# Half of a pair's softmax blocks stay where they are: four block transfers in place of six, a copy back on two engines, a doubled buffer, and the value product 1.9 heads later

## The chip, the cores and the metric

The kernel runs on one NeuronCore of a Trainium2 chip. The metric is the device time of one execution in microseconds (us). The core has a matmul engine (PE; its weight loads are listed apart as PEld), a vector engine (DVE), a scalar engine (ACT), a general engine (POOL) and a queue engine (SP), which issues every DMA of this kernel. Each engine takes its instructions strictly in the order in which they were written out.

## The reference

The inputs are `q`, `k`, `v` of 8 batches, 8 heads, 576 tokens and 64 channels, and `s` of 8 x 8 x 576. First a causal attention with a decay bias, then a gated feed-forward block on its output:

```python
cum  = cumsum(max(s, 0))
bias = -(cum[i] - cum[j])
scores = where(j > i, -1e9, q @ k.T / 8 + min(bias, 0))
attn = softmax(scores)
x    = (attn @ v).transpose(0, 2, 1, 3).reshape(8, 576, 512)

h = gelu_tanh(x @ w_in);  u, v = halves(h)         # 576 x 512 each
v_n  = layer_norm(v) * g_ln
gated = u * (w_sg @ v_n + b_sg)                    # w_sg is 576 x 576, over tokens
return x + gated @ w_out
```

All of it is in 32-bit floating point; products in the fast 32-bit format split each operand into a high and a low part and use three matmuls for one.

## The kernel before, in words

**Heads and pairs.** There are 64 heads, worked on in 32 pairs. For one head (`scores`, line 949) the 576 queries are cut into five tiles of 64 or 128 rows, in an order of tokens that `_tokens` (line 1221) lays out from the table `BLK` (line 38), so that the five tiles need only 64, 192, 320, 448 and 576 keys each. The matmuls of a tile go to a PSUM bank (`sc`, or `sx` for the widest). Then `softmax` (line 918) runs three steps on each tile: DVE adds the mask and takes the row extreme (`mn`), ACT takes the exponential and the row sum, and DVE transposes the tile in blocks of 32 x 32 into the SBUF buffer `ex`.

**The buffers ex and pt.** After the block transpose, the 32 queries of a block lie along the columns and 32 keys along the partitions. A quarter of the partitions (32) holds one block of queries. `ex` has two halves of 1600 columns: keys whose block of 32 is even lie in the first, odd ones in the second. The product with `v` wants 64 keys on 64 neighbouring partitions. So for each pair `shuffle` (line 973) moves all eight pieces of 32 partitions x 1600 columns from `ex` to a second buffer `pt`, in six transfers issued by SP, two of which carry 64 partitions. There is one `ex` and one `pt`: the transposes of the next pair wait until the transfers have read `ex`, and the next transfers wait until the matmuls have read `pt`.

**The product with v.** `pv` (line 991) issues one uninterrupted group of 76 matmuls for a pair (38 pieces from `pieces`, line 978, each as two instructions of 64 x 64), reading `pt` and `v`, into two PSUM banks `xx`. Then four DVE multiplications scale the result by the reciprocal row sums `rb` and write `xr`, the input of the feed-forward block. The sums take a path of their own (`scales`, line 936): ACT and DVE make the reciprocals, DVE transposes them to `rt`, a DMA writes `rd` in DRAM, and two DMAs read it back spread over the partitions as `rb`. `rb` and `v` have one buffer each.

**The feed-forward block.** For each batch `ffn` (line 1014) issues units of 12 or 14 matmuls: `v_unit` (`vm`), `u_unit` (`um`), `s_unit` (`sm`) and `o_unit` (`om`), each followed by steps on ACT, DVE and POOL. The tag `u2` with `U2` = 8 buffers holds the `u` results, two small operands `xq`, the output tiles `ot`, and at the start the weights in preparation. All PSUM work but `sx` shares six banks.

**What sets the order.** Nothing is issued as the code runs. Every step is noted with a key in units of heads: for head h the loads at h - 2, the split of its operands at h - 1, the scores at h, and for the second head of a pair the shuffle at h + 0.0 and `pv` at h + 0.2 (`POS`, line 58); the feed-forward block of batch b lies between 8b + 10 and 8b + 17.6. A planner (`plan`, line 553) with a cost for each instruction (`cost`, line 382) then writes one fixed order for each engine: of the operations that are ready first by its costs, the one with the lowest key, moved by a table `SHIFT` (line 73) that has a row for each kind of operation. The keys are priorities, not times. All instructions leave through one helper, line 532, so the profile shows that line for all of them, and the work is told apart by tile names.

**Number formats.** Heads 0 to 11 use plain 32-bit matmuls with operands straight from DRAM (`kf`); later heads load `raw` and split it on ACT and POOL into `k` and `low`.

Of the kernel before, what the change touches and what calls it, by code (L numbers as in the profile page):

```python
# [18 lines left out]
BH = B * H  # L19
# [18 lines left out]
BLK = ((0, 1, 4, 5, 8), (-1, 2, 3, 6, 7))  # L38
# [12 lines left out]
U2 = 8  # L51
# [6 lines left out]
POS = dict(load=-2.0, split=-1.0, sc=(0, 0, 0, 0), sh=0.0, pv=0.2, wv=(0.1, 7.5),  # L58
# [8 lines left out]
LATENCY = [[54, 38, 39, 80, 60], [54, 35, 33, 77, 60], [54, 34, 35, 90, 60], [55, 34, 35, 80, 60], [1060] * 5]  # L67
# [3 lines left out]
ISSUE = {"pt": 645.0, "rb": 660.0, "rd": 620.0, "xq": 690.0, "kf": 580.0, "vnr": 590.0, "low": 320.0}  # L71
PHASE = (4.0, 9.0, 13.5, 61.5)
SHIFT = {
# [4 lines left out]
    "act activation sum 128x10 sum": (-10.5, 10.85, -13.42, -6.92, -0.94),  # L78
# [4 lines left out]
    "act activation vnr 64x512 vm": (-0.36, 10.23, 2.64, 2.87, -17.42),  # L83
# [4 lines left out]
    "act activation wbits 128x256 wraw": (6.84, 39.64, 82.81, 1.09, 0.4),  # L88
    "act copy cc 64x576 cf": (-0.29, 1.38, -0.29, -0.29, 0),
    "act copy cf 64x512 cps": (-4.37, -9.03, -1.53, -0.95, 0),  # L90
    "act copy cf 64x64 cps": (7.84, 7.54, 7.6, 7.91, 5.93),
    "act copy gt 128x288 u": (9.81, 3.71, 1.85, -0.84, 0),
    "act copy k 128x576 raw": (0, 0, 77.83, 273.57, 108.47),
    "act copy k 64x576 raw": (3.7, -1.3, 3.65, 9.4, 3.91),
    "act copy low 64x576 raw": (0, 0, 0.07, 0.07, -0.05),
    "act copy vt 64x512 vm": (-16.19, -21, -55.46, -44.19, -10.31),
    "act copy wi 128x256 wbits": (23, 16.76, 25.17, 25.17, 9.38),
    "act copy wo 128x256 wbits": (4.72, 6.23, 184.14, 7.43, 5.62),
    "act copy wr 128x576 wst": (-1.42, 0.68, 0.68, -2, 1.47),
    "act copy wr 1x576 wst": (0, 0.15, 0, 0.07, 0.57),  # L100
    "act copy ws 128x576 wst": (-30.29, -30.57, -26.17, -23.47, -24.47),
# [6 lines left out]
    "dve memset low 2x1152 -": (-3.2, -1.71, -1.4, 0.26, 0),  # L108
    "dve memset maska 128x64 -": (-7.53, 8.57, -3.85, 6.42, 9.89),
    "dve memset maskb 128x448 -": (0, 0, 1.51, -0.11, -0.11),  # L110
    "dve memset maskc 128x576 -": (0.13, 1.82, -3.47, -5.95, -11.1),
    "dve memset sum 128x1 -": (-0.23, -0.23, -0.23, 0.3, 0.3),
    "dve memset sum 128x52 -": (4.68, -7.24, -2.73, 9.64, 9.97),
    "dve memset vnr 33x512 -": (-0.01, 1.25, 8.26, 8.26, 4.22),
# [3 lines left out]
    "dve reciprocal sum 128x10 sum": (-0.44, 3.06, 0.25, -0.33, -3.42),  # L118
# [8 lines left out]
    "dve scalar_tensor_tensor wbits 128x256 wraw": (0, -9.07, 330.04, 137.29, 35.9),  # L127
    "dve scalar_tensor_tensor wm 128x256 wraw": (134.99, 306.62, 40.25, 11.65, 28.53),
# [3 lines left out]
    "dve tensor_scalar wbits 128x256 wbits": (-3.2, -1.01, 18.81, -10.4, 1.45),  # L132
    "dve tensor_scalar wm 128x256 wbits": (66.01, 167.25, -0.39, -4.28, -4.47),
    "dve tensor_tensor cf 64x512 cps": (2.84, 0.59, 1.89, 7.81, 0),
    "dve tensor_tensor cf 64x64 cps": (1.88, 1.2, -7.04, -10.79, -0.86),
# [3 lines left out]
    "dve tensor_tensor vnr 64x512 vm": (13.68, 14.78, 14.83, 9.99, -2.48),  # L139
# [12 lines left out]
    "dve transpose rt 128x32 sum": (-14.48, 10.59, 55.5, -72.28, -2.17),  # L152
# [198 lines left out]
class Program:  # L351
# [30 lines left out]
    def cost(self, op):  # L382
# [5 lines left out]
        d, load, port, gap = 50.0, 0.0, 0.0, 0.0  # L388
        if e == PE:
            if name == "group":  # L390
                d, load = 3000.0, 54.0
            else:
                w, m = ins
                load, n = 0.84 * w.columns(), m.columns()
# [884 lines left out]
```

## Time and profile before

| what | value |
|---|---|
| median of 3 runs | 859.82 us (856.74 to 873.91) |
| profiled execution | 855.12 us, span from the first to the last instruction 853.4 us |
| mean granted clock of PE | 0.926 of 2.4 GHz |
| DMA traffic | 123.74 MB, mean 145 GB/s |
| chain that ended last | PE 41%, DMA 27%, DVE 15%, SP's queue 6%, ACT 4% |

The chain is the work followed back from the last instruction, at each step to what released it. A busy engine is one that executes; matmuls are pipelined, so the sum of their single durations exceeds their busy time. The profiled execution took 1.7 us more than its span and is 4.7 us below the median.

### The profile page before, as it was taken

How to read it: one execution, taken by the hardware profiler on the slowest of the kernel's cores; microseconds unless marked ns; L12 is line 12 of the kernel's file. 1: busy time of each engine (PE TensorE's matmuls, PEld its weight loads, DVE VectorE, ACT ScalarE, POOL GpSimd, SP SyncE). 2: the span in 40 equal slices, each digit the busy share in tenths (PEclk: the TensorE clock that was granted, in tenths of full speed). 3: DMA queues.
4: the chain of work that ended last, by engine and by line, in shares of the span. 5: the costliest groups of instructions: out<-in, count | busy, mean ns of one | idle time of the engine just before them, and what ended most of it. 6: DMA issues, size and time to landing. Idle time of an engine off the chain costs nothing.

```text
span 853.4 us, 17656 instructions
## 1 busy us (share of the span) xinstructions
PE 720.7 (84%) x6114; PEld 643.8 (75%) x6114; DVE 576.8 (68%) x1722; ACT 496.8 (58%) x1258; POOL 442.1 (52%) x611
## 2 busy tenths in 40 slices
PE   7666684898988897888987899898986889789998
PEld 5444453888877886787876888787976889688998
DVE  6657658875678648775677667785678657683562
ACT  4443456775677556775567656784567656661440
POOL 7123368763555734556445634665445635534641
PEclk9776797899999999999999999999998999999999
DMA  7577885555555665545655456545664564544101
GB/s 182 155 194 199 224 218 147 143 148 152 157 149 150 170 165 120 144 107 159 178 157 149 122 149 175 149 114 162 171 157 106 144 171 132 138 114 94 48 29 56
DMA packets 70097, 123.74 MB, mean 145 GB/s; under 512 B 20996, under 2 KB 45700, under 8 KB 70008
## 3 DMA queue, kind: packets, MB, share of 16 engines
q1 hardware_dynamic: 70008, 122.61, 54.8%
q8 instruction: 49, 0.80, 0.4%
q14 instruction: 40, 0.33, 0.1%
HBM read 56.72 MB, written 10.26 MB: 78 GB/s over the span
## 4 chain that ended last, share of the span: by engine, by line
PE 41%; DMA 27%; DVE 15%; SPq 6%; ACT 4%; issue 3%; POOL 3%; DVEq 0%; POOLq 0%; ACTq 0%
PE om L532 9%; DMA pt<-ex 9%; PE xx L532 7%; DMA rb<-rd 7%; PE um L532 7%; SPq L532 6%; DMA rd<-rt 6%; PE vm L532 6%; PE sm L532 5%; PE sc L532 4%; DVE ex L532 3%; DVE sc L532 3%; PE sx L532 3%; DMA kf<-in_kf 2%; DVE u L532 2%
## 5 line engine op out<-in xcount | busy, mean ns | idle before, releaser
L532 ACT ACTIVATE sc<-sc,mn 128x448 f32<-128x448 f32 (+3 forms) x256 | 112.8, 440 | 112.6 <-DVE mn L532 107.3
L532 PE MATMUL xx<-pt,v 64*64 64x256 f32 (+4 forms) x2432 | 122.0, 351 | 63.8 <-DMA pt<-ex 54.9
L532 PEld LDWEIGHTS xx<-pt,v 64*64 64x64 f32 x2432 | 106.9, 160 | 81.6 <-issue 57.3
L532 DVE STREAM_TRANSPOSE ex<-sc 64x64 f32<-64x64 f32 (+3 forms) x256 | 106.5, 430 | 79.3 <-DMA pt<-ex 38.4
L532 POOL TENSOR_TENSOR k<-raw,k 64x576 fp32r<-64x576 f32 x52 | 73.6, 1416 | 134.5 <-ACT k L532 114.7
L532 PE MATMUL sm<-ws,vn 128*128 128x288 f32 x768 | 125.3, 299 | 3.6 <-ACT vn L532 3.1
L532 PE MATMUL om<-gt,wo 128*128 128x288 f32 x768 | 117.8, 301 | 6.1 <-ACT gt L532 3.1
L532 PE MATMUL um<-xs,wi 128*128 128x288 f32 x768 | 119.8, 302 | 1.5 <-DVE xr L532 1.5
L532 PE MATMUL vm<-wi,xs 128*128 128x512 f32 (+1 forms) x416 | 115.3, 409 | 2.6 <-POOL xs L532 2.4
L532 ACT CAST k<-raw 128x576 fp32r<-128x576 f32 x156 | 104.6, 670 | 22.1 <-DMA raw<-in_kq 9.0
L532 PEld LDWEIGHTS om<-gt,wo 128*128 128x128 f32 x768 | 108.7, 192 | 9.5 <-ACT gt L532 4.1
L532 PEld LDWEIGHTS sm<-ws,vn 128*128 128x128 f32 x768 | 108.7, 189 | 5.2 <-ACT vn L532 3.6
L532 PEld LDWEIGHTS um<-xs,wi 128*128 128x128 f32 x768 | 109.5, 193 | 3.4 <-PE sx L532 2.1
L532 PEld LDWEIGHTS vm<-wi,xs 128*128 128x128 f32 (+1 forms) x416 | 76.0, 190 | 18.9 <-POOL xs L532 3.4
L532 POOL TENSOR_TENSOR low<-raw,k 64x576 fp32r<-64x576 f32 x52 | 73.9, 1421 | 5.7 <-ACT k L532 2.9
L532 POOL TENSOR_TENSOR gt<-u,gt 128x288 fp32r<-128x288 f32 x64 | 50.2, 805 | 49.2 <-ACT gt L532 34.3
L532 DVE CUSTOM_DVE_ANT_0 sc<-sc,maskb 128x192 f32<-128x192 f32 (+1 forms) x128 | 62.3, 492 | 14.3 <-PE sc L532 13.9
L532 DVE SCALAR_TENSOR_TENSOR u<-u,um 128x288 f32<-128x288 f32 x128 | 55.7, 442 | 16.0 <-ACT u L532 15.0
L532 DVE SCALAR_TENSOR_TENSOR ot<-om,xr 128x288 f32<-128x288 f32 x64 | 28.7, 454 | 54.8 <-PE om L532 51.6
L532 ACT CAST low<-raw 64x576 fp32r<-64x576 f32 x52 | 34.9, 671 | 46.9 <-DMA raw<-in_kq 46.0
L532 PE MATMUL sc<-k 128*128 128x320 f32 x208 | 58.3, 286 | 4.4 <-DVE xr L532 4.3
L532 DVE TENSOR_TENSOR xr<-xx,rb 128x128 f32<-128x128 f32 (+1 forms) x128 | 31.4, 298 | 43.8 <-DMA rb<-rd 35.7
(102 smaller groups left out, 1355.8 us busy)
## 6 DMA issues: line engine op xcount, KB each, us to landing
pt<-ex SPq DMA_DIRECT2D x64, 400.0 KB
pt<-ex SPq DMA_DIRECT2D x128, 200.0 KB
v<-in_vp SPq DMA_DIRECT2D x32, 576.0 KB
raw<-in_kq SPq DMA_DIRECT2D x52, 288.0 KB
rb<-rd SPq DMA_DIRECT2D x64, 160.0 KB
out_t<-ot SPq DMA_DIRECT2D x64, 144.0 KB
wraw<-in_w_in SPq DMA_DIRECT2D x16, 256.0 KB
kf<-in_kf SPq DMA_DIRECT2D x11, 292.5 KB
```

The costliest lines, as they stand in the source:

```text
L532: real[i] = [getattr(op["eng"].real, name)(*[f(a) for a in args], **{k: f(v) for k, v in kw.items()}).ins for args, kw in calls]
```

## The change

- `ex` holds two pairs (four halves of 1600 columns), `pt` one half instead of two. The half to write is chosen by the pair's parity (`base`).
- `shuffle` moves four pieces instead of eight: two transfers from `ex` to `pt`, then two within `ex` over the pieces that were just saved, then ACT and POOL each copy one saved piece from `pt` to the place in `ex` that came free. Four pieces never move.
- `pv` reads `ex`, and its key is h + 1.9 instead of h + 0.2. The five query tiles' order of tokens (`BLK`, `_tokens`), the layout of `v` and the masks change with the new places; the pieces that had 32 columns of their own join the first wide one, so a group has 34 pieces, 68 instructions. The four DVE multiplications become two.
- The transposed reciprocals are written into a corner of `rb` instead of `rt`.
- `U2` is 5 instead of 8.
- The planner's DMA costs and the table `SHIFT` are new, so each engine's order is new as well.

```diff
-BLK = ((0, 1, 4, 5, 8), (-1, 2, 3, 6, 7))
+BLK = ((0, 1, 3, 6, 8), (-1, 2, 4, 5, 7))
-U2 = 8
+U2 = 5
-POS = dict(load=-2.0, split=-1.0, sc=(0, 0, 0, 0), sh=0.0, pv=0.2, wv=(0.1, 7.5),
+POS = dict(load=-2.0, split=-1.0, sc=(0, 0, 0, 0), sh=0.0, pv=1.9, wv=(0.1, 7.5),
...
-    xt_ = const.tile([P, 2 * RG], F32, name="ex")
-    pt_ = const.tile([P, 2 * RG], F32, name="pt")
-    nc.gpsimd.memset(xt_[64:P].pattern(0, (RG, 2), (49 * 32, 2), (1, 32)), 0.0)
+    xt_ = const.tile([P, 4 * RG], F32, name="ex")
+    pt_ = const.tile([P, RG], F32, name="pt")
+    nc.gpsimd.memset(xt_[64:P].pattern(0, (RG, 4), (49 * 32, 2), (1, 32)), 0.0)
...
-        nc.vector.transpose(out=xt_[0:r].pattern(32 * cell(h % 2, it, 0), (32, n), (RG, 2), (1, 32)), in_=o)
+        nc.vector.transpose(out=xt_[0:r].pattern(base(h) + 32 * cell(h % 2, it, 0), (32, n), (RG, 2), (1, 32)), in_=o)
+    def base(h):
+        return h // 2 % 2 * 2 * RG
...
-        rt = att.tile([P, 32], F32, name="rt", tag="rt", bufs=1)
-        nc.vector.transpose(out=rt, in_=rs)
+        rb = scale_rows[h // 2] = att.tile([P, 640], F32, name="rb", tag="rb", bufs=1)
+        nc.vector.transpose(out=rb[:, 320:352], in_=rs)
         rd = dram.tile([P, 32], F32, name="rd", tag="rd", bufs=2)
-        nc.sync.dma_start(out=rd, in_=rt)
-        rb = scale_rows[h // 2] = att.tile([P, 640], F32, name="rb", tag="rb", bufs=1)
+        nc.sync.dma_start(out=rd, in_=rb[:, 320:352])
...
     def shuffle(h):
-        for o, i, n, a, b in ((1, 0, 2, 0, 1), (1, 2, 2, 1, 1), (0, 0, 1, 0, 0), (0, 2, 1, 1, 0), (3, 1, 1, 0, 0), (3, 3, 1, 1, 0)):
-            nc.sync.dma_start(out=pt_[32 * o:32 * (o + n), RG * a:RG * a + RG],
-                              in_=xt_[32 * i:32 * (i + n), RG * b:RG * b + RG])
+        qs = [slice(32 * q, 32 * q + 32) for q in range(4)]
+        a, b = (slice(base(h) + RG * i, base(h) + RG * i + RG) for i in range(2))
+        for o, i in ((1, 0), (2, 3)):
+            nc.sync.dma_start(out=pt_[qs[o], :], in_=xt_[qs[i], a])
+        for o, i in ((0, 1), (3, 2)):
+            nc.sync.dma_start(out=xt_[qs[o], a], in_=xt_[qs[i], b])
+        nc.scalar.copy(out=xt_[qs[1], b], in_=pt_[qs[1], :])
+        nc.gpsimd.tensor_scalar(out=xt_[qs[2], b], in0=pt_[qs[2], :], scalar1=1.0, scalar2=1.0, op0=ALU.mult, op1=ALU.mult)
...
-            if m is None:
-                o, x = to.pattern(0, (1, 32)), pt_[rows].pattern(32 * cell(z, 0, 0), (1, 32))
-            else:
-                o = to.pattern(32 * m, (128, 2), (1, 32 * n))
-                x = pt_[rows].pattern(32 * cell(z, m, j), (RG, 2), (32 * (10, -12)[z], n), (1, 32))
+            o = xx[g][64 * z:64 * z + 64].pattern(32 * (m - g), (160 - 32 * g, 2), (1, 32 * n))
+            x = xt_[rows].pattern(base(h) + (1 - g) * RG + 32 * cell(z, m, j), ((-RG, RG)[g], 2), (32 * (10, -12)[z], n), (1, 32))
...
-        for g in range(2):
-            for c0, o, n in ((0, 160 * g, 160), (160, 160 * g + 352, 128)):
-                nc.vector.tensor_tensor(out=xt[:, CH * g + c0:CH * g + c0 + n], in0=xx[g][:, c0:c0 + n],
-                                        in1=rb[:, o:o + n], op=ALU.mult)
+        nc.vector.tensor_tensor(out=xt[:, 0:320], in0=xx[0][:, 0:320], in1=rb[:, 0:320], op=ALU.mult)
+        nc.vector.tensor_tensor(out=xt.pattern(320, (128, 2), (1, 128)), in0=xx[1].pattern(0, (128, 2), (1, 128)),
+                                in1=rb.pattern(352, (160, 2), (1, 128)), op=ALU.mult)
...
```

## Rows read from the trace of the kernel before

**Rows 1.** Page, part 1: busy us, share of the span, instructions.

```profile
PE 720.7 (84%) x6114; PEld 643.8 (75%) x6114; DVE 576.8 (68%) x1722; ACT 496.8 (58%) x1258; POOL 442.1 (52%) x611
```

**Rows 2.** Busy time by stage: stretch, length, engines, clock, DMA share, GB/s.

```profile
core 0: us, PE busy (x) PEld busy (x) DVE busy (x) ACT busy (x) POOL busy (x), PEclk, DMA share, GB/s
0.00:150.00 150.00, 98.55 (x628) 70.82 (x629) 100.77 (x319) 72.47 (x205) 74.04 (x104) 0.80 0.71 188
150.00:750.00 600.00, 526.42 (x4723) 482.08 (x4724) 421.82 (x1274) 390.75 (x975) 327.96 (x437) 0.95 0.57 148
750.00:853.00 103.00, 95.69 (x768) 90.91 (x766) 54.19 (x131) 33.61 (x80) 40.11 (x72) 0.98 0.24 64
```

**Rows 3.** Waits of PE, 150 to 750 us: us in total, times, longest.

```profile
PE xx L532 <- DMA pt<-ex: 46.2, 24, 11.0
PE sx L532 <- DVE ex L532: 13.0, 9, 4.2
PE xx L532 <- DVE mn L532: 4.1, 2, 2.1
PE xx L532 <- DMA raw<-in_kq: 2.4, 1, 2.4
```

**Rows 4.** Busy time around one pair's shuffle.

```profile
358.00:364.00 6.00, 3.27 (x30) 2.88 (x28) 5.94 (x15) 5.78 (x13) 4.36 (x8) 1.00 1.01 233
364.00:369.00 5.00, 4.71 (x72) 4.37 (x73) 2.12 (x6) 1.31 (x6) 2.70 (x4) 0.66 0.34 96
```

**Rows 5.** PE in order of time, groups of xx: start us, duration us.

```profile
150.62 4.20 PE L532 MATMUL xx<-pt,v 64*64 64x32 f32 x72 [0.23 <-DMA pt<-ex]
...
311.50 2.87 PE L532 MATMUL xx<-pt,v 64*64 64x32 f32 x76 [1.34 <-DMA pt<-ex]
...
754.02 4.63 PE L532 MATMUL xx<-pt,v 64*64 64x32 f32 x76 [1.06 <-DMA pt<-ex]
```

**Rows 6.** SP in order of time, the same pair: start us, us, issues.

```profile
355.11 3.92 SPq L532 DMA_DIRECT2D pt<-ex  x6
359.13 1.38 SPq L532 DMA_DIRECT2D rd<-rt  x1
...
364.36 1.34 SPq L532 DMA_DIRECT2D rb<-rd  x2
```

**Rows 7.** Chain that ended last, 355 to 400 us: start us, us, what.

```profile
358.43 5.72 DMA pt<-ex
...
386.49 5.00 DMA rd<-rt
```

**Rows 8.** Waits of all engines, whole run: three of DVE.

```profile
DVE ex L532 <- DMA pt<-ex: 38.4, 15, 4.4
...
DVE xr L532 <- DMA rb<-rd: 35.7, 17, 5.9
...
DVE ex L532 <- DMA out_t<-ot: 13.4, 5, 3.9
```

**Rows 9.** Groups by shape: count, busy us, mean ns, idle before, releaser.

```profile
L532 PE MATMUL xx<-pt,v 64*64 64x256 f32 x640 | 67.1, 477 | 6.0 <-DMA pt<-ex 5.8
...
L532 PE MATMUL xx<-pt,v 64*64 64x32 f32 x256 | 14.6, 234 | 57.9 <-DMA pt<-ex 49.1 <-DVE mn L532 4.1 <-DMA raw<-in_kq 2.4
...
L532 DVE TENSOR_TENSOR xr<-xx,rb 128x160 f32<-128x160 f32 x64 | 20.0, 317 | 43.8 <-DMA rb<-rd 35.7 <-PE xx L532 4.1 <-PE sx L532 2.3
...
L532 DVE TENSOR_TENSOR xr<-xx,rb 128x128 f32<-128x128 f32 x64 | 15.5, 278 | 0.0
...
L532 ACT CAST k<-raw 64x576 fp32r<-64x576 f32 x104 | 69.8, 671 | 4.4 <-POOL k L532 2.4
...
L532 ACT CAST gt<-u 128x288 fp32r<-128x288 f32 x64 | 26.0, 430 | 23.1 <-PE om L532 13.0 <-DVE u L532 9.5
...
L532 POOL TENSOR_SCALAR xs<-xr 128x576 fp32r<-128x576 f32 x32 | 21.1, 673 | 41.1 <-DVE xr L532 26.5 <-issue 12.2 <-DMA kf<-cf 1.6
```

**Rows 10.** Waits of PE, 0 to 150 us.

```profile
PE xx L532 <- DMA pt<-ex: 18.6, 5, 11.0
```

**Rows 11.** Waits of SP's queue, whole run.

```profile
SPq L532 <- DMA rd<-rt: 57.6, 26, 4.2
```

More of the change, by code (lines that the diff above doesn't have):

```diff
@@ L65 @@
 METHODS = {"tensor": PE, "scalar": ACT, "vector": DVE, "gpsimd": POOL, "sync": SP}
-LATENCY = [[54, 38, 39, 80, 60], [54, 35, 33, 77, 60], [54, 34, 35, 90, 60], [55, 34, 35, 80, 60], [1060] * 5]
+LATENCY = [[54, 38, 39, 80, 60], [54, 35, 33, 77, 60], [54, 34, 35, 90, 60], [55, 34, 35, 80, 60], [150] * 5]
 OVERLAP = [0, 93, 75, 25, 0]
@@ L70 @@
 MARGIN = 58.17
-ISSUE = {"pt": 645.0, "rb": 660.0, "rd": 620.0, "xq": 690.0, "kf": 580.0, "vnr": 590.0, "low": 320.0}
+ISSUE = {"pt": (640.0, 205.0), "ex": (640.0, 205.0), "rb": (700.0, 82.0), "rd": (540.0, 82.0), "xq": (690.0, 160.0),
+         "kf": (580.0, 220.0), "vnr": (590.0, 200.0), "low": (320.0, 270.0), "ot": (440.0, 490.0)}
 PHASE = (4.0, 9.0, 13.5, 61.5)
 SHIFT = {
[4 rows of a table removed]
-    "act activation sum 128x10 sum": (-10.5, 10.85, -13.42, -6.92, -0.94),
[4 rows of a table removed]
-    "act activation vnr 64x512 vm": (-0.36, 10.23, 2.64, 2.87, -17.42),
[4 rows of a table removed]
[L88 to L101, printed above, removed]
[6 rows of a table removed]
[L108 to L114, printed above, removed]
[3 rows of a table removed]
-    "dve reciprocal sum 128x10 sum": (-0.44, 3.06, 0.25, -0.33, -3.42),
[8 rows of a table removed]
-    "dve scalar_tensor_tensor wbits 128x256 wraw": (0, -9.07, 330.04, 137.29, 35.9),
-    "dve scalar_tensor_tensor wm 128x256 wraw": (134.99, 306.62, 40.25, 11.65, 28.53),
[3 rows of a table removed]
[L132 to L135, printed above, removed]
[3 rows of a table removed]
-    "dve tensor_tensor vnr 64x512 vm": (13.68, 14.78, 14.83, 9.99, -2.48),
[12 rows of a table removed]
-    "dve transpose rt 128x32 sum": (-14.48, 10.59, 55.5, -72.28, -2.17),
[37 rows of a table removed]
-    "pool affine_select maska 32x64 maska": (95.51, -4.49, -29.07, -17.03, 4.24),
-    "pool affine_select maskb 32x448 maskb": (-3.27, -3.42, 4.16, -16.76, -12.09),
-    "pool affine_select maskc 32x576 maskc": (-48.42, -0.32, -0.35, -2.73, 17.03),
-    "pool affine_select tri 128x576 tri": (-25.84, -32.9, -20.28, 0, -20.21),
-    "pool memset ex 64x128 -": (-3.29, -4.07, -4.1, 7.93, 2.34),
-    "pool memset tri 128x576 -": (32.91, -6.22, -6.84, 4.19, -0.39),
[4 rows of a table removed]
-    "pool tensor_scalar wbits 128x256 wbits": (-2.96, 9.08, -45.78, -0.18, 0.59),
[5 rows of a table removed]
-    "pool tensor_tensor k 64x576 raw": (-0.92, 1, 1.07, -0.21, -0.92),
-    "pool tensor_tensor low 64x576 raw": (-5.11, -4.49, -26.18, 100.59, -21.54),
-    "pool tensor_tensor vn 128x512 vt": (-5.7, 21.24, -29.42, -3.14, -4.88),
-    "pool tensor_tensor wi 128x256 wbits": (1.2, 1.79, 2.21, 2.21, 0.83),
-    "pool tensor_tensor wo 128x256 wbits": (-29.73, 1.86, 257.42, 76.47, 9.99),
-    "pool tensor_tensor wr 1x576 wst": (0.01, 0.01, -0.19, -5.07, 0),
-    "pool tensor_tensor wr 64x576 wst": (-2.76, -8.06, -5.49, -9.53, 2.58),
-    "pool tensor_tensor ws 128x576 wst": (37.65, -19.35, -51.61, -6.54, 4.97),
[7 rows of a table removed]
-    "sp dma_start low 2x1152 cum": (4.5, 5.95, 7.01, 15.55, 4.94),
[7 rows of a table removed]
-    "sp dma_start vnr 64x512 vnr": (6.52, 5.78, -0.73, 10.9, 11.59),
[5 rows of a table removed]
[3 rows of a table added]
+    "act activation sum 128x10 sum": (3.82, 4.66, 56.12, 17.35, -22.13),
[4 rows of a table added]
+    "act activation vnr 64x512 vm": (3.38, 3.38, 3.38, 3.38, 3.32),
[4 rows of a table added]
+    "act activation wbits 128x256 wraw": (12.81, 23.31, 15.24, 2.91, -3.04),
+    "act copy cc 64x576 cf": (30.8, -15.97, -15.84, -27.85, 8.96),
+    "act copy cf 64x512 cps": (6.82, 6.95, 2.72, 1.33, 1.98),
+    "act copy cf 64x64 cps": (-12.23, -12.25, 0.77, -3.6, 17.45),
+    "act copy ex 32x1600 pt": (2.11, 2.11, 8.19, 0.96, -0.15),
+    "act copy gt 128x288 u": (6.65, 1.97, 4.65, 11.04, 4.74),
+    "act copy k 128x576 raw": (-8.09, 6.2, -1.34, 101.2, 0.56),
+    "act copy k 64x576 raw": (5.62, 5.49, 15.59, 99.03, 9.86),
+    "act copy low 64x576 raw": (12.89, 12.94, 12.94, 0.06, -5.16),
+    "act copy vt 64x512 vm": (-8.41, -2.47, -2.5, -5.05, -5.92),
+    "act copy wi 128x256 wbits": (-0.48, 5.93, -3.16, 3.66, -17.79),
+    "act copy wo 128x256 wbits": (-14.55, 8.67, 10.51, -13.27, 9.97),
+    "act copy wr 128x576 wst": (0, -2.7, -2.97, -2.88, -0.18),
+    "act copy wr 1x576 wst": (-12.69, -14.66, -18.24, -15.87, -18.2),
+    "act copy ws 128x576 wst": (-13.38, -11.05, -21.02, -1.37, -1.37),
[6 rows of a table added]
+    "dve memset low 2x1152 -": (2.18, 1.59, -4.4, -13.47, 5.93),
+    "dve memset maska 128x320 -": (0.83, 0.03, 3.82, 1.89, 0.62),
+    "dve memset maskb 128x576 -": (-0.22, 0.2, 0.2, -0.22, -0.22),
+    "dve memset sum 128x1 -": (-5.69, -7.9, -7.65, -6.26, -6.98),
+    "dve memset sum 128x52 -": (-11.23, 7.01, 0.55, 0.74, 0.74),
+    "dve memset vnr 33x512 -": (2.86, -3.96, 1.53, -17.46, -2.87),
[3 rows of a table added]
+    "dve reciprocal sum 128x10 sum": (14.09, 0.44, 0.44, 35.34, 6.22),
[8 rows of a table added]
+    "dve scalar_tensor_tensor wbits 128x256 wraw": (21.38, 401.09, 479.36, 32.46, 4.06),
+    "dve scalar_tensor_tensor wm 128x256 wraw": (-0.27, 23.24, 7.77, 3.95, -17.56),
[3 rows of a table added]
+    "dve tensor_scalar wbits 128x256 wbits": (8.88, 9.16, 9.78, 8.76, 14.56),
+    "dve tensor_scalar wm 128x256 wbits": (-2.1, -4.14, -2.29, 0.66, -7.01),
+    "dve tensor_tensor cf 64x512 cps": (-3.06, -3.1, -3.1, -3, 0.44),
+    "dve tensor_tensor cf 64x64 cps": (1.34, 2.73, -6.56, -0.12, 0.75),
[3 rows of a table added]
+    "dve tensor_tensor vnr 64x512 vm": (-15.81, -14.94, -9.7, 9.53, -7.16),
[11 rows of a table added]
+    "dve transpose rb 128x32 sum": (0.03, 0.03, 0.03, 0, -0.11),
[36 rows of a table added]
+    "pool affine_select maska 128x320 maska": (20.47, 20.46, 23.3, 37.02, 17.85),
+    "pool affine_select maskb 64x576 maskb": (0.74, 0.74, 0.74, 0.84, 6.57),
+    "pool affine_select tri 128x576 tri": (0, 0.28, 0, 0, -2.22),
+    "pool memset ex 64x256 -": (90.59, 7.5, 15.91, 7.96, 2.48),
+    "pool memset tri 128x576 -": (3.23, 2.82, 2.79, 2.58, -4.95),
[3 rows of a table added]
+    "pool tensor_scalar wbits 128x256 wbits": (-0.11, -0.11, -0.11, -0.22, -0.22),
[5 rows of a table added]
+    "pool tensor_tensor k 64x576 raw": (0, -3.5, 57.87, 6.64, 1.05),
+    "pool tensor_tensor low 64x576 raw": (-17.36, -23.73, 11.14, 89.43, 0),
+    "pool tensor_tensor vn 128x512 vt": (-0.35, -2.16, 7.53, 8.48, -0.28),
+    "pool tensor_tensor wi 128x256 wbits": (4.2, 6.11, 10.07, 22.21, 13.1),
+    "pool tensor_tensor wo 128x256 wbits": (3.77, -3.23, -4.44, -2.5, -10.18),
+    "pool tensor_tensor wr 1x576 wst": (-4.42, 0.17, -6.04, -18.92, -11.27),
+    "pool tensor_tensor wr 64x576 wst": (-1.99, -13.7, 66.98, -16.05, -9.31),
+    "pool tensor_tensor ws 128x576 wst": (-1.35, -2.41, -3.2, -6.37, -5.24),
[8 rows of a table added]
+    "sp dma_start low 2x1152 cum": (-16.97, -14.24, 0, 0, 0),
[6 rows of a table added]
+    "sp dma_start vnr 64x512 vnr": (3.8, -4.4, -0.39, 0, -2.26),
[5 rows of a table added]
@@ L390, in cost @@
             if name == "group":
-                d, load = 3000.0, 54.0
+                d, load = 2750.0, 54.0
             else:
@@ L439, in cost @@
             r = v.dims[0][1]
-            d = r * v.columns() * 4 / 300.0
-            load = ISSUE.get("".join(c for c in v.buf.name if not c.isdigit()), 440.0)
+            load, rate = ISSUE.get("".join(c for c in v.buf.name if not c.isdigit()), (440.0, 270.0))
+            d = r * v.columns() * 4 / rate
         if e in (ACT, DVE) and any(v.off[1] for v in outs + big if v.columns() > 1):
@@ L647, in plan @@
                 s = max(s, flight[-8])
-            moved = max(moved, s + 800) + d
-            free[e], end = s + load, moved + 600
-            flight.append(end + 1060)
+            moved = max(moved, s + 850) + d
+            free[e], end = s + load, moved + 750
+            flight.append(end)
         else:
@@ L789, in tile_attn_gmlp @@
     masks = []
-    for i, w in enumerate((64, 448, 576)):
-        m = const.tile([P, w], BF16, name="mask" + "abc"[i])
+    for i, w in enumerate((320, 576)):
+        m = const.tile([P, w], BF16, name="mask" + "ab"[i])
         nc.vector.memset(m, 0.0)
-        for q in range(4):
-            c = (32 * q, w - 128 + 64 * (q % 2 == (i == 1)) + 32 * (q // 2))[i > 0]
-            x = m[32 * q:32 * q + 32, :]
-            nc.gpsimd.affine_select(out=x, in_=x, pattern=[[-1, w]], base=c, channel_multiplier=1,
+        for r0, r1, c in (((0, P, w - 128),), ((0, 64, w - 64), (64, P, w - 128)))[i]:
+            nc.gpsimd.affine_select(out=m[r0:r1, :], in_=m[r0:r1, :], pattern=[[-1, w]], base=c, channel_multiplier=1,
                                     compare_op=ALU.is_ge, fill=NEG)
@@ L921, in softmax @@
         o = pst[0:r, c0:c0 + w]
-        m = masks[(0, 1, 2, 1, 2)[it]][0:r]
+        m = masks[it > 2][0:r]
+        c = m.columns() - w if it else 192
         mn = d["mn"][0:r, it:it + 1]
-        nc.vector.tensor_tensor_reduce(out=o, in0=o, in1=m[:, m.columns() - w:m.columns()], scale=-0.125, scalar=3.0e38,
+        nc.vector.tensor_tensor_reduce(out=o, in0=o, in1=m[:, c:c + w], scale=-0.125, scalar=3.0e38,
                                        op0=ALU.add, op1=ALU.min, accum_out=mn)
@@ L981, in pieces @@
             at = 0
-            for z in range(2):
-                todo.append((at, g, z, 0, None, 0))
             for j in range(BLK[g][4] + 1):
-                m = next(it for it in range(1, 5) if BLK[g][it] >= j)
-                for z in range(2):
-                    todo.append((at + 0.5, g, z, j, m, 5 - m))
+                m = next(it for it in range(5) if BLK[g][it] >= j)
+                todo += [(at, g, z, j, m, 5 - m) for z in range(2)]
                 at += 5 - m
-        return sorted(todo, key=lambda x: (x[0], x[1], x[2]))
+        return sorted(todo, key=lambda x: x[:3])
     def pv(h):
@@ L997, in pv @@
         for _, g, z, j, m, n in pieces():
-            rows, to = slice(64 * g, 64 * g + 64), xx[g][64 * z:64 * z + 64]
-            if m is None:
-                o, x = to.pattern(0, (1, 32)), pt_[rows].pattern(32 * cell(z, 0, 0), (1, 32))
-            else:
-                o = to.pattern(32 * m, (128, 2), (1, 32 * n))
-                x = pt_[rows].pattern(32 * cell(z, m, j), (RG, 2), (32 * (10, -12)[z], n), (1, 32))
-            calls.append(((o, v[rows, z, j, :], x), dict(start=j == 0, stop=m is None or j == BLK[g][4])))
+            rows = slice(64 * g, 64 * g + 64)
+            o = xx[g][64 * z:64 * z + 64].pattern(32 * (m - g), (160 - 32 * g, 2), (1, 32 * n))
+            x = xt_[rows].pattern(base(h) + (1 - g) * RG + 32 * cell(z, m, j), ((-RG, RG)[g], 2), (32 * (10, -12)[z], n), (1, 32))
+            calls.append(((o, v[rows, z, j, :], x), dict(start=j == 0, stop=j == BLK[g][4])))
         nc.group(calls)
         rb = scale_rows.pop(h // 2)
-        for g in range(2):
-            for c0, o, n in ((0, 160 * g, 160), (160, 160 * g + 352, 128)):
-                nc.vector.tensor_tensor(out=xt[:, CH * g + c0:CH * g + c0 + n], in0=xx[g][:, c0:c0 + n],
-                                        in1=rb[:, o:o + n], op=ALU.mult)
+        nc.vector.tensor_tensor(out=xt[:, 0:320], in0=xx[0][:, 0:320], in1=rb[:, 0:320], op=ALU.mult)
+        nc.vector.tensor_tensor(out=xt.pattern(320, (128, 2), (1, 128)), in0=xx[1].pattern(0, (128, 2), (1, 128)),
+                                in1=rb.pattern(352, (160, 2), (1, 128)), op=ALU.mult)
         del heads[h], heads[h - 1]
@@ L1222, in _tokens @@
     import numpy as np
-    rows, cols = [2 * BLK[g][t] + z for t in range(1, 5) for z in range(2) for g in range(2)] + [0, 1], []
+    rows, cols = [2 * BLK[g][t] + q for t in range(1, 5) for g in range(2) for q in range(2)] + [0, 1], []
     for g in range(2):
-        cols += [g] + [2 * BLK[g][t] + z for z in range(2) for t in range(1, 5)]
+        cols += [2 * BLK[g][t] + q for q in range(2) for t in range(g, 5)]
     return [(np.array(x)[:, None] * 32 + np.arange(32)).ravel() for x in (rows, cols)]
@@ L1241, in _layout @@
     kf = np.concatenate([kf, row], axis=1)
-    v9 = v.reshape(BH // 2, 2, 9, 2, 32, D)[:, :, :, (0, 1, 1, 0)]
+    v9 = v.reshape(BH // 2, 2, 9, 2, 32, D)[:, :, :, (1, 0, 0, 1)]
     s_t = np.concatenate([i["s"].reshape(BH, S).T, np.zeros((5 * P - S, BH), i["s"].dtype)])
```

220 rows, old and new, of the table SHIFT are left out of this document.

## The prediction

> **What bounds the kernel now.** I began with the busy shares of the page: PE is busy 84% and no other engine over 68% [rows 1], so PE is the engine to fill, yet it is idle for 133 us. The table by stage says where [rows 2]. Up to 150 us, almost with attention alone, PE is busy 98.6 of 150 us at a mean clock of 0.80. From 150 to 750 us, where attention and feed-forward interleave, it is idle 600 - 526.4 = 73.6 us at 0.95. After 750 us it is nearly full.
>
> The waits of PE in the middle stage name the cause [rows 3]. The groups of xx waited 46.2 us for the shuffle's transfers and 6.5 us more for DVE or another DMA named as last; the scores sx waited 13.0 us for the transposes into ex, which in their turn stand behind the shuffle: DVE waited 38.4 us for pt<-ex [rows 8]. One pair shows how it happens. SP needs 3.92 us to issue six transfers [rows 6], and the last lands 5.72 us after its issue [rows 7], so 9 us pass from the first issue to the group. At the end of that, from 358 to 364 us, the DMA engines are full (share 1.01, 233 GB/s) while PE is busy 3.27 of 6 us; from 364 to 369 us PE is busy, but at 0.66 of its clock [rows 4].
>
> That is the second loss. The group of 76 takes 2.87 us where PE had been kept busy, and 4.2 to 4.6 us after a longer wait [rows 5]. Of the 27 groups from 150 us on I count 14 that took 4.0 to 4.6 us, the first and last of them shown, and 13 of 2.6 to 3.1 us. The clock has two levels, 1.2 and 2.4 GHz; at the lower the whole stretch after a wait runs slowly.
>
> **The change, part by part.** The sum is made against the profiled execution, 855.1 us, which is 0.5% below the median of 859.8 us; 2% around that median, 842.6 to 877.0 us, is about what a measurement can tell from no change.
>
> *pv at h + 1.9 and ex doubled.* In the middle stage 46.2 + 4.1 + 2.4 = 52.7 us of PE's waits stand before xx [rows 3]. The shuffle of a pair now has about 1.9 heads to land, over 20 us, since pairs stand (754.0 - 150.6)/25 = 24.1 us apart [rows 5], and the next pair's transposes go to the other halves. I take away 39 us; the other 14 us I leave, since a queue that no longer stalls here meets another engine's lateness sooner. Bounds: 0 and 53 us. Of the 13.0 us before sx I take 8 (0 to 13): the cause goes, but sx then stands behind DVE's other work.
>
> *The clock.* Fourteen slow groups cost 14 x (4.3 - 2.87) = 20 us over fast ones [rows 5]; I take 16 (0 to 20). The matmuls that follow the group in the same slow stretch would gain too; I leave them out for idle gaps that remain. The Trainium skill, "TensorE: Matmul & The Clock Gate", section "Terms", prices it otherwise, as the time spent at the low level times one half: a mean of 0.95 over 600 us means 60 us at half clock, hence 30 us instead of 16, by which the sum would be 14 us lower. The rows decide for the smaller, because a part of the slow time in rows 4 is time without work.
>
> *Fewer pieces.* Eight instructions of 32 columns go, 14.6 us / 256 = 57 ns each, together 0.46 us a group; four of 256 columns become 320, at 67.1 us / 640 = 105 ns by at most a quarter more, 0.1 us [rows 9]. The number of columns is unchanged, so the gain lies between 0 and 0.36 us a pair. I take 0.25 x 32 = 8 us, as PE is the path in most of the run.
>
> *Fewer multiplications.* Four on DVE, 2 x 317 + 2 x 278 = 1190 ns, become one of 320 and one of 256 columns. By the slope of 39 ns for 32 columns [rows 9] these are 512 and 434 ns: 8 us of DVE in all, off the path. DVE's 35.7 us of waiting for rb [rows 8] should go, as the sums too have 20 us now. New is that the transposed reciprocals go into rb itself, so the next pair's wait for these two multiplications, placed 0.1 heads ahead of them, and the queue behind them on DVE (masks, transposes) waits with them if pv slips.
>
> *The copies.* An ACT cast of 576 columns takes 671 ns and one of 288 takes 430 ns [rows 9]; 1600 columns are then 671 + 1024 x 0.84 = 1.53 us. POOL's one-input operation takes 673 ns for 576 columns, so 1.5 us with ACT's fixed share and 1.87 us in proportion. That is 49 us more on ACT (497 to 546 us) and 49 to 60 us on POOL (442 to about 495 us). Behind ACT's copy stand exponentials and gelu steps. ACT is busy 65% of the middle stage [rows 2], which covers it; if that cover goes at the faster pace, 49 us is the upper bound. I charge 8.
>
> *Transfers and SP.* Four issues of about 0.65 us instead of six free 1.3 us a pair on SP, and the moved bytes halve, 1.6 MB to 0.8 MB a pair. But the second two transfers can only be issued when the first two have landed, and the copies wait for the second. Two landings of 5 to 5.7 us [rows 7], four issues and a copy make about 14 us against 9 now, within 20 us and so nothing in the middle. In front of the last batch's feed-forward it is 5 us more, under what is left of the batch before; I charge 2 (0 to 5). The load of v, in one buffer, now follows a pv that is 1.7 heads later, and still has two heads.
>
> *U2 = 5.* Eight u, eight ot and two xq a batch pass through five buffers. The nearest row is DVE's 13.4 us in five waits for out transfers with eight [rows 8]. I charge 2 and keep 0 to 13. Masks and memsets differ only under the first loads: nothing.
>
> *The start.* Up to 150 us the groups waited 18.6 us for pt [rows 10], but PE is not the path there; loads and DVE share it. I take 10 (0 to 19).
>
> The sum: 855.1 - 39 - 8 - 16 - 8 - 10 + 8 + 2 + 2 = 786 us. PE would be busy about 697 of 784 us, 89%, which the last stage passes already (95.7 of 103, [rows 2]). With the waits, the clock and the pieces at their upper ends and 8 us of costs it would be 855.1 - 53 - 13 - 20 - 12 - 10 + 8 = 755 us.
>
> **The rivals.** *The next engine takes the place of the wait.* At 786 us ACT would have 546 us and DVE 569 us of work, 69% and 72%, as averages over stages; between 150 and 750 us DVE's 422 and ACT's 391 + 40 us would fall into some 535 us, 79 and 81%, in fixed orders whose real times differ from the planned ones. For it speaks that from 358 to 364 us DVE and ACT are full just when PE waits (5.94 and 5.78 of 6 us, [rows 4]): part of PE's wait for the shuffle is also a wait for them. Then half of the first two and of the clock comes back: 786 + 31 = 817, with the copies at a half of their bound 834 us.
>
> *Nothing that can be measured.* The wait goes from pt to another name: the group is late anyway, since the reciprocals or v come late, or the shuffle has hidden behind DVE. Only the shorter groups remain, about 850 us. Against it: the wait's releaser is the transfer itself in 24 of these 27 cases [rows 3].
>
> *Slower: SP stands still.* The wait for the first two transfers happens on SP's queue, and whatever was written behind it (a head's raw, the rd and rb of the sums, output tiles) waits too. It does so already for rd, 57.6 us in 26 waits [rows 11]. The price is a landing a pair, 5 to 5.7 us [rows 7], or 32 x 5.35 = 171 us of SP. The issues of rows 6 take 6.6 us of a pair's 24, so SP has room; the point of decision is whether over half of it, 91 us, reaches the chain: 786 + 91 is 877. At 60% it is 889 us. The Trainium skill, "DMA: Bandwidth & Descriptors", section "Anatomy of one DMA", says that a transfer's semaphore wait is served on the issuing sequencer before dispatch; rows 11 agree with it, since they show that wait on SP. Against this rival: the planner may write other transfers between the two rounds, and the first two need not wait for bytes that no longer move.
>
> **How the numbers follow.** The forecast, a time below 815 us and most likely near 786, gets 0.62; the next engine, 815 to 842 us, 0.19; no measurable change 0.11; SP's queue 0.08. The range of 755 to 843 us holds the forecast but for 0.02 below it, and the second case: 0.79. Faster by over 2% is the first two, 0.81; the same 0.11; slower 0.08.
>
> **What would show it.** Right: no wait of xx for a transfer over 1 us in the middle stage, groups of 68 near 2.6 us in nearly all pairs, DVE's waits for pt and rb gone, a mean clock there of at least 0.98, pairs 21 to 22 us apart, DMA traffic near 97 MB. Copies of 1.5 us on ACT and POOL with the exponentials' waits no longer than before. The next engine: PE's waits under ACT or DVE names at 30 us or more. SP: a wait of 5 us a pair for pt<-ex on SP's queue, followed by ACT waiting for raw or DVE for rb. Wrong altogether: xx waiting for ACT's or POOL's copy, or the span unchanged with the clock still at 0.95.

## The result, and the profile after

The changed kernel takes 761.4 us (median; 759.2 to 762.6) against 859.9 us: a ratio of 0.887 (95% interval 0.8835 to 0.8905). The profiled execution took 762.6 us with a span of 760.9 us.

The busy shares of the page of the changed kernel, as [rows 1]:

```profile
PE 692.3 (91%) x5858; PEld 620.5 (82%) x5858; DVE 577.5 (76%) x1657; ACT 536.8 (71%) x1290; POOL 485.7 (64%) x634
```

PE lost 720.7 - 692.3 = 28.4 us of busy time and (853.4 - 720.7) - (760.9 - 692.3) = 64.1 us of idle time; that is the whole difference of the spans. By stage, as [rows 2], where the middle stage ends earlier:

```profile
0.00:150.00 150.00, 107.71 (x746) 83.97 (x746) 117.50 (x351) 91.53 (x240) 87.29 (x118) 0.85 0.65 168
150.00:660.00 510.00, 488.73 (x4355) 446.05 (x4356) 404.01 (x1175) 405.06 (x961) 352.67 (x444) 0.97 0.48 130
660.00:761.00 101.00, 95.91 (x759) 90.51 (x757) 55.97 (x134) 40.23 (x92) 45.70 (x74) 1.00 0.21 59
```

In the middle stage PE is idle 21.3 us, where it was 73.6, and DVE and ACT stand at 79%. The longest waits of PE in that stage, as [rows 3]:

```profile
PE sx L528 <- DVE ex L528: 11.2, 7, 2.1
PE sc L528 <- DVE vnr L528: 4.2, 1, 4.2
```

No wait of xx is left in this stage. Up to 150 us it is otherwise: there the groups wait for the copies, 18.1 us in all, where they had waited 18.6 us for pt [rows 10], and four of the six groups that begin there take 5.1 to 5.9 us. The waits of PE for xx, 0 to 150 us:

```profile
PE xx L528 <- ACT ex L528: 13.8, 4, 5.5
...
PE xx L528 <- DVE ex L528: 4.3, 1, 4.3
```

One pair in order of time (start, duration, queue or engine), as [rows 5] and [rows 6]:

```profile
406.55 1.21 SPq L528 DMA_DIRECT2D pt<-ex  x2
...
409.96 0.51 SPq L528 DMA_DIRECT2D ex<-ex  x1
...
411.19 0.51 SPq L528 DMA_DIRECT2D ex<-ex  x1
...
413.68 0.36 PE L528 MATMUL sx<-k 128*128 128x256 f32 x1 [2.09 <-DVE ex L528]
...
415.21 1.53 ACT L528 COPY ex<-pt 32x1600 f32<-32x1600 f32 x1
...
417.28 3.13 PE L528 MATMUL xx<-ex,v 64*64 64x320 f32 x68
```

From the first issue to the group pass 10.7 us, not the 14 us I had reckoned: 3.4 us from the first issue to the first of the second round, 4.0 us from the last issue to the copy. Yet the group comes half a microsecond after the copy. From 150 us on the copies end at most 1.4 us ahead of the group in 19 of 26 pairs and 3.9 to 5.8 us ahead in 7. The key h + 1.9 did not give the transfers 20 us; it moved the group behind other work in PE's order, so that PE has something to do in these 10 us. No group after 150 us took more than 3.3 us; most took 2.72 us.

The group shown took 3.13 us because the clock was low: from 414.8 to 418.1 us the granted clock was 0.50, the lower of its two levels. Between 170 and 660 us it fell five times, each time at the end of, or right behind, a wait of 2.1 us before sx such as the one shown. These five make up nearly all of the 11.2 us of that wait.

### The profile page after: what moved, and what is told of

Same layout as the page of the kernel before. It is cut to its first block, busy times and chain, and to the rows that moved or that the text cites. A ratio compares the mean times of both kernels' runs of the same rounds, so it can differ in the third digit from the quotient of the medians.

```text
span 760.9 us, 16999 instructions
## 1 busy us (share of the span) xinstructions
PE 692.3 (91%) x5858; PEld 620.5 (82%) x5858; DVE 577.5 (76%) x1657; ACT 536.8 (71%) x1290; POOL 485.7 (64%) x634
## 4 chain that ended last, share of the span: by engine, by line
PE 48%; DVE 12%; DMA 10%; ACT 9%; POOL 6%; issue 3%; SPq 0%; POOLq 0%; DVEq 0%; ACTq 0%
PE sm L528 10%; PE vm L528 9%; PE om L528 9%; PE xx L528 8%; PE um L528 7%; DMA raw<-in_kq 4%; PE sc L528 3%; DVE ex L528 3%; ACT sc L528 2%; DMA pt<-ex 2%; PE sx L528 2%; ACT k L528 2%; DVE sc L528 2%; DMA out_t<-ot 2%; DVE u L528 1%
## 5 line engine op out<-in xcount | busy, mean ns | idle before, releaser
L528 ACT ACTIVATE sc<-sc,mn 64x64 f32<-64x64 f32 (+3 forms) x256 | 112.4, 439 | 42.1 <-DVE mn L528 39.2
L528 PE MATMUL sm<-ws,vn 128*128 128x288 f32 x768 | 130.3, 307 | 0.4 <-DVE ex L528 0.2
L528 PE MATMUL xx<-ex,v 64*64 64x128 f32 (+4 forms) x2176 | 100.3, 334 | 18.1 <-ACT ex L528 13.8
L528 PEld LDWEIGHTS xx<-ex,v 64*64 64x64 f32 x2176 | 87.2, 146 | 35.5 <-ACT ex L528 16.5
L528 PEld LDWEIGHTS sm<-ws,vn 128*128 128x128 f32 x768 | 113.5, 196 | 2.6 <-DVE ex L528 1.2
L528 DVE CUSTOM_DVE_ANT_0 sc<-sc,maska 128x192 f32<-128x192 f32 (+2 forms) x192 | 66.8, 355 | 15.4 <-PE sc L528 14.2
L528 POOL TENSOR_SCALAR ex<-pt 32x1600 f32<-32x1600 f32 x32 | 48.9, 1529 | 39.7 <-DMA ex<-ex 30.9
L528 PE MATMUL sc<-k 128*128 128x320 f32 (+1 forms) x208 | 60.3, 300 | 6.9 <-DVE vnr L528 4.2
L528 DVE TENSOR_TENSOR xr<-xx,rb 128x320 f32<-128x320 f32 x64 | 27.0, 447 | 50.1 <-PE xx L528 50.1
L528 ACT CAST gt<-u 128x288 fp32r<-128x288 f32 x64 | 25.8, 429 | 54.0 <-DVE u L528 42.7
```

Of the source, the lines that this page charges most:

```text
L528: real[i] = [getattr(op["eng"].real, name)(*[f(a) for a in args], **{k: f(v) for k, v in kw.items()}).ins for args, kw in calls]
```

## The experiments

In nearly all of these SHIFT is emptied, since the first pair of runs showed that at each kernel's own key it matters little. Times are medians, with the ratio to the kernel before on the same chip. The e, f and g runs stood on three chips; distances between them, taken by the ratios instead of the times, come out up to 4 us otherwise.

**The order tables.** Both kernels with `SHIFT = {}`.

> The changed kernel with its table SHIFT emptied, so that the planner orders by keys alone. Theory A (the room between shuffle and product and the second half of ex give the gain; the order table only polishes): 770 to 790 us, no wait of xx for a transfer over 1 us, and some 95 us below the kernel before with its table emptied. Theory B (the gain is the newly written order, fitted to this kernel): 815 us or more, and under 45 us from the kernel before with its table emptied.

> The kernel before with its table SHIFT emptied; the other end of the comparison. Theory A: 865 to 885 us, with PE still waiting about 55 us for pt. Theory B: little to lose here or there, 855 to 865 us, the changed one then near it.

Measured: 765.0 us (0.886, 0.884 to 0.889) and 852.7 us (0.989, 0.987 to 0.991). The distance is 87.7 us without either table, so theory B falls. Theory A's numbers were off at both ends: 765.0 us is 5 us under its range, and the kernel before gains 1% without its table where it was to lose some. What e1 keeps of the new order is the planner's new costs; those of the DMAs have a run of their own below.

**One number of the change alone, tables kept.** `pv=1.9` in the kernel before, `pv=0.2` in the changed one.

> The kernel before with one number changed: the product with v at h + 1.9 in place of h + 0.2. Still one ex, six transfers, pt occupied until the product. Theory A, in the form that the distance takes PE's waits away and the second half of ex those of DVE: 800 to 830 us, xx waiting under 10 us for pt, but DVE's wait of ex for pt at 38 us or more. Rival (without the second half the distance is worth nothing, because the transposes of the next pair hold PE's scores instead): 845 to 870 us, with the waits of sx and sc for DVE's ex at 40 us or more.

> The changed kernel with the product back at h + 0.2. Theory A: the shuffle of two rounds and a copy stands in front of the product again, some 14 us; PE's waits of xx return, 50 us or more under the names of ACT's and POOL's copies, clock near 0.93: 830 to 865 us. Rival (the second half of ex is what counts, since DVE and PE can go on with the next pair whatever the product waits for): 765 to 795 us.

Measured: 887.8 us (1.030, 1.026 to 1.034) and 878.8 us (1.020, 1.016 to 1.024): both slower than the kernel before and outside every expectation. The table of each kernel is fitted to its own key, so both were run again without it.

**The same moves without tables.** One number in each kernel, SHIFT emptied in both.

```diff
 # f5, in the kernel before                 # f6, in the changed kernel
-POS = dict(..., pv=0.2, ...                -POS = dict(..., pv=1.9, ...
+POS = dict(..., pv=1.9, ...                +POS = dict(..., pv=0.2, ...
```

> The kernel before with SHIFT emptied and the product at h + 1.9: the earlier run of this move kept a table fitted to the key 0.2. Theory A2 (with one ex the distance buys nothing, since the next pair's transposes still wait for the transfers and pt is held until the product): 845 to 875 us. Rival (the earlier slowdown was the ill-fitting table, the distance alone is worth half the gain): 790 to 820 us.

> The changed kernel with SHIFT emptied and the product back at h + 0.2, two pairs in ex. Theory A2 (the second half buys nothing without the distance, as xx stands in PE's order behind a chain of two rounds and a copy): 835 to 875 us, xx waiting 60 us or more for copies. Rival (the ill-fitting table again): 770 to 800 us.

Measured: 836.5 us (0.974, 0.970 to 0.979) and 845.2 us (0.983, 0.978 to 0.988). So an ill-fitting table had cost 51 and 34 us. The first time lies under theory A2's range and far over the rival's, the second in A2's range. Distance alone gives 852.7 - 836.5 = 16 us of the 88, so A2's "buys nothing" was too strong. With one ex DVE stays behind the transfers, and PE with it, as the waits of f5 show:

```profile
DVE ex L370 <- DMA pt<-ex: 77.0, 26, 7.4
PE xx L370 <- DMA pt<-ex: 39.2, 18, 5.6
...
PE sx L370 <- DVE ex L370: 24.0, 17, 3.0
```

In f6 PE waits for the copies instead, as theory A2 said, if less than the 60 us it named:

```profile
PE xx L371 <- ACT ex L371: 43.0, 16, 6.0
```

**Transfers in place with one ex**, at h + 0.2 and without the table.

```diff
     def base(h):
-        return h // 2 % 2 * 2 * RG
+        return 0
```

> The changed kernel with SHIFT emptied, the product at h + 0.2 and only one pair in ex (the base column is always 0): what is left of the change is four transfers in place, the two copies, 68 instructions, two multiplications, U2 = 5 and the planner's DMA costs. Theory A2: the longer chain is now in the path of both the product and the next pair's transposes, 880 to 920 us. Rival (half the bytes and fewer issues are a gain by themselves): 830 to 852 us.

Measured: 903.6 us (1.053, 1.047 to 1.058). Half the bytes and a third fewer issues are no gain here, taken together with what else the run holds (the two copies, U2 = 5, the planner's costs); how much each of these has in it, the run does not tell. The waits of PE in f7 show the chain of two rounds and a copy in its path:

```profile
PE xx L371 <- ACT ex L371: 80.1, 24, 6.2
```

The second half of ex is then worth 903.6 - 845.2 = 58 us at h + 0.2, and the distance 845.2 - 765.0 = 80 us on top of it. The distance with one ex and transfers in place was not run.

**U2 = 5 in the kernel before** (`-U2 = 8`, `+U2 = 5`).

> The kernel before with SHIFT emptied and U2 = 5 in place of 8. My term of 2 us (0 to 13): 852 to 858 us. Rival (a u unit without a buffer holds a PSUM bank and PE stands): 868 us or more.

Measured: 863.3 us (1.005, 1.002 to 1.008), 10.6 us over the same kernel with eight. In f8 the scores sx waited longer for DVE's transposes than the 9.4 us of e2:

```profile
PE sx L370 <- DVE ex L370: 22.1, 17, 2.5
```

The time lies between the two expectations. The price, 10.6 us, or 14 us by the ratios, is at the upper end of my bounds of 0 to 13 us and far from the 2 us I took. That the longer wait of sx is the price is read from its size alone.

**The planner's DMA costs alone**, in the kernel before without its table: LATENCY, ISSUE, and the lines of `cost` and `plan` for SP.

> The kernel before with SHIFT emptied and only the planner's DMA costs of the changed kernel (latency, issue and rate by tile); six transfers, one ex, product at h + 0.2. Theory A3 (the costs only polish; PE waits because nothing stands in its order that it could do while the transfers run): 840 to 865 us, xx still waiting 40 us or more for pt. Rival (PE waits because the old costs let the planner put the group too early): 800 to 825 us, xx waiting under 20 us.

Measured: 838.9 us (0.972, 0.964 to 0.979), 14 us better than 852.7. Just under theory A3's range, far from the rival's; the 33.4 us of xx below lie between the 40 us and the 20 us that the two had named. The four runs of g1 lie further apart than others (831.7 to 843.4 us), so the 14 us are rough. The waits of PE in g1 show why it is no more: xx waits half as long as the 65.7 us of e2, and sm waits instead.

```profile
PE xx L371 <- DMA pt<-ex: 33.4, 22, 5.7
PE sm L371 <- DVE vnr L371: 29.6, 8, 4.9
```

**Without the copies back**: the lines `nc.scalar.copy(out=xt_[qs[1], b], ...)` and `nc.gpsimd.tensor_scalar(out=xt_[qs[2], b], ...)` taken out.

> The changed kernel with SHIFT emptied and without the two copies back from pt to ex: the product reads two blocks that are not in their place, so this part of the computation is left out. 49 us of ACT and 49 us of POOL go. My term of 8 us for them: 752 to 760 us against 765. If the copies are hidden altogether: 762 to 768 us. Rival (ACT at 80% in the middle stage is the next bound): 740 us or less.

Measured: 742.2 us (0.862, 0.859 to 0.865), 22.8 us under e1: between my term of 8 us and the rival. The busy shares of g2, to be held against 687.9 us of PE, 534.6 of ACT and 487.9 of POOL in e1, show 43 us less on ACT, 49 us less on POOL and 7 us less on PE:

```profile
PE 680.9 (92%) x5858; PEld 611.7 (83%) x5858; DVE 565.8 (77%) x1657; ACT 491.6 (66%) x1258; POOL 438.5 (59%) x602
```

The other 16.6 us are idle time of PE. The run also takes the copies out of the chain in front of the group, so it does not tell the engines' load from that latency. But e1 has only 8.5 us of PE waiting for the copies before xx (8.3 for ACT's, 0.2 for POOL's), so that wait alone is not the 22.8 us.

**A version meant to beat both**: `tag="xr", bufs=7` and `U2 = 7`.

> The changed kernel with SHIFT emptied, one of the eight xr buffers given up and two more buffers for u2 bought with it (7 and 7). Five u2 buffers cost the kernel before 10.6 us. If they cost the same here and the eighth xr buffer is spare: 753 to 759 us, under both kernels. If u2 no longer stands in the way, or xr does: 764 to 780 us.

Measured: 781.9 us (0.908, 0.904 to 0.911), 17 us slower than e1 and just outside the slower of the two ranges. Its middle stage by engines (PE first) lacks 15 us of PE's work against the 485.2 us of e1 in the same stretch:

```profile
150.00:660.00 510.00, 470.46 (x4184) 425.08 (x4185) 379.04 (x1124) 389.82 (x920) 338.29 (x419) 0.99 0.46 125
```

The eighth xr buffer is not spare, or the two u2 buffers changed the order for the worse; one run does not tell which.

**How far the product must move**: `pv=1.1`.

> The changed kernel with SHIFT emptied and the product at h + 1.1, after the next head's scores but ahead of the one after. In the trace of the changed kernel the group starts 9 to 17 us after the first transfer's issue, so the key 1.9 is a place in PE's order rather than 20 us. Theory A3 (what counts is that other work with a lower key stands ahead of the group; one head's is enough): 762 to 785 us. Rival (the gain grows with the distance): 800 to 825 us, half-way between 845 at 0.2 and 765 at 1.9.

Measured: 813.6 us (0.945, 0.942 to 0.948), on the rival's side: theory A3, that one head's work ahead of the group is enough, falls. The waits of PE in g4:

```profile
PE xx L371 <- ACT ex L371: 33.3, 16, 3.1
```

I counted, from 150 us on, the groups that came within 0.06 us of their copies' end, or were partly issued ahead of it: 14 of 26 at h + 0.2 (f6), 17 at h + 1.1 (g4), 4 at h + 1.9 (e1). Groups that took more than 3.5 us were 13, 10 and 1. At 1.1 the group of these 17 pairs still stands at the head of PE's order when the copies end, so a delay of the chain is PE's. Against e1, g4 has (810.0 - 700.7) - (763.1 - 687.9) = 34 us more of idle PE and 700.7 - 687.9 = 13 us more of busy time.

## Why the prediction was right, and where its sizes were off

The direction and the cause hold from 150 us on: PE waited for the shuffle, and there the wait and the slow groups behind it are gone. DVE's wait of ex for pt fell from 38.4 us [rows 8] to 0.4 us in the whole run:

```profile
DVE ex L528 <- DMA pt<-ex: 0.4, 1, 0.4
```

Its waits for rb are gone, pairs stand 21 us apart and the DMA traffic is 97.5 MB, as I had named for being right. Missed are the mean clock, 0.97 for at least 0.98, and the first 150 us: there xx waits for the copies, the sign I had put down for being wrong altogether.

The sum of 786 us was 24.6 us too high. The time lies 6 us above the lower end of the range. That end takes waits, clock and pieces at their upper ends and only 8 us of costs. If the costs below hold, the gains went beyond those ends and larger costs hid it, so that the time lies inside is in part luck. By its terms:

- *Waits before xx:* I took 39 of 52.7 us and left 14 us for other lateness. All went in the middle stage, and the idle time there fell by 73.6 - 21.3 = 52.3 us. This is the term whose size was furthest off among the gains.
- *Scores sx:* 8 us taken, 13.0 - 11.2 = 1.8 us gained. What is left is still DVE's lateness, as I had half suspected, and the five falls of the clock stand behind it.
- *Clock and pieces:* 16 + 8 = 24 us against 28.4 us of busy time. The groups' busy time fell from 122.0 to 100.3 us; at full clock a group went from 2.87 to 2.72 us, 0.15 in place of 0.25 us. The mean clock rose from 0.95 to 0.97 in the middle stage and from 0.80 to 0.85 up to 150 us. So the pieces are 32 x 0.15 = 4.8 us of the 28.4, and 23.6 us are left for the clock, where I took 16. My reading of rows 5 was wrong in one point: I put the slow groups down to longer waits, but there a group took 2.87 us after a wait of 1.34 us and another 4.63 us after 1.06 us, so the length of the wait before a group does not tell whether it is slow. The Trainium skill, "TensorE: Matmul & The Clock Gate", section "Terms", prices the clock as the time at the low level times one half. An estimate by that rule from the means of both traces is 0.05 x 600 - 0.03 x 510 = 15 us in the middle and 0.20 x 150 - 0.15 x 150 = 7.5 us at the start. The 23.6 us agree with the 22 us of that estimate within the rounding of the means. Rows 4 do not bear out my reason for the smaller price: there the idle stretch has a granted clock of 1.00, and in the slow one PE is busy 4.71 of 5 us. Not all of the 30 us that the rule gave for the middle stage came back, since the clock did not reach 1.
- *Start:* 10 us taken, of the 18.6 us of waits for pt; idle time up to 150 us fell from 51.5 to 42.3 us, and 746 matmuls were done by then in place of 628. The number came true by luck: the groups still wait 18.1 us there, so the 9.2 us come from other waits, and which part of the change took them away no run shows.
- *Copies:* 1.53 us on each engine, as worked out, but 22.8 us of time where I charged 8. *U2:* 10.6 us in the kernel before where I charged 2. Both costs were too small. If they hold in the changed kernel, the gains were larger still than the sum of the terms says; which term held them, no run shows.
- *Multiplications:* 487 and 407 ns, near the 512 and 434 of the slope.
- *The next engine* did reach the shares I gave (79% measured for both; I had 79% for DVE and 81% for ACT), but PE's waits under the names of DVE and ACT in the middle stage come to some 19 us, under the 30 us I had named. What the load costs beyond named waits is the open part of the copies' 22.8 us. *SP's queue* waited for pt 21.3 us in 26 times, the longest 2.1 us, where the rival needed 5 us a pair; in the pair shown, rd is issued between the two rounds. The wait, over the whole run:

```profile
SPq L528 <- DMA pt<-ex: 21.3, 26, 2.1
```

What I had wrong in the mechanism is the 20 us: from 150 us on the group begins 9 to 17 us after its first transfer's issue, where it began 8 to 11 us after it before. The key decides what stands ahead of it. And the parts are not a sum: from 852.7 us, distance alone gives 16 us, in-place transfers with one ex cost 51 us (with U2 and the planner's costs), the second half of ex returns 58 us, and then the distance is worth 80 us. Each without the other leaves DVE or PE in front of the same chain, as f5 and f6 show. What the in-place transfers are good for I only argue: with them two pairs fit into 5 column blocks of 1600 (4 before; two pairs with six transfers would want 6).

Open is how the 22.8 us of the copies divide between load and latency, and what U2 = 5 costs in the changed kernel. Two rivals were not run: two pairs in ex with the six transfers, which would tell whether the transfers in place are needed at all, and one ex at h + 1.9 with the new planner's costs. f5 kept the old costs, so its 16 us for the distance alone may be too small.

## What to carry to other kernels

When a fixed order makes an engine wait for a transfer, ask first what that engine and its feeders could do meanwhile: a later place in the order and a second buffer may each be worth little (here 16 us, and 7.5 us with all the rest of the change), and both together ten per cent. A longer chain that nobody waits for beats a shorter one in the path. And a table of fitted offsets must be emptied or fitted again before one number of the schedule is tried alone, or its misfit (34 and 51 us here) hides the answer.

## What the runs showed of the hardware that I had not expected

In the chain that ended last, a transfer of 32 partitions took 2.7 to 4.0 us from issue to landing, where the last of six took 5.72 us [rows 7] while the DMA engines were full [rows 4]. ACT and POOL take the same 1529 ns (mean of 32 each) for a copy of 32 partitions x 1600 columns:

```profile
L528 POOL TENSOR_SCALAR ex<-pt 32x1600 f32<-32x1600 f32 x32 | 48.9, 1529 | 39.7 <-DMA ex<-ex 30.9 <-DVE vt L528 3.9 <-ACT sc L528 2.3
L528 ACT COPY ex<-pt 32x1600 f32<-32x1600 f32 x32 | 48.9, 1529 | 11.8 <-DMA ex<-ex 11.2
```
